# Three expert tiles that start from six batches' routing, the earliest one's layer 1 queued around the last router's steps

## The chip, the cores and the metric

One core of a Trainium2 chip runs one program that holds attention, routing and a mixture of experts. The metric is the device time of one execution in microseconds, as the median of several runs. The engines named below are PE (TensorE, matmuls; it loads weights on a track of its own), DVE (VectorE), ACT (ScalarE), POOL (GpSimd) and SP (SyncE, which here only issues DMAs).

## The reference

```
# q, k, v: 8 batches x 8 heads x 1152 x 64
q_pool = q.reshape(B, H, 576, 2, 64).mean(axis=3)
attn   = softmax(q_pool @ k^T / 8)            # 576 x 1152 for each head
x      = (attn @ v) laid out as 4608 tokens x 512
logits = x @ w_gate                            # 8 experts
e      = argmax(logits, axis=1)                # one expert for each token
scale  = softmax(logits)[e] * sigmoid(x @ w_output_gate)[e]
out    = scale * (relu(x @ w1[e]) @ w2[e])     # 512 -> 1024 -> 512
```

Everything is float32; the kernel keeps that precision by splitting operands into a high and a low part (`...h`, `...l`) and multiplying the parts.

## The kernel before

**Attention.** 32 pairs of heads (8 batches x 4 pairs) go through PE one after another. For each pair there is a pass for the row maxima (`mp`), then 18 score tiles (`sps`), each turned on ACT into `p` and `ph`, and on POOL or DVE into the remainder `pl` (L411, L405), then P V (`av`, L426 to L428). DVE normalises the result into `xb` (`norm`, L435 to L437). After each pair, `logits` transposes that part of `xb` (L481), splits it and multiplies it with the gate weights (L498). After a batch's fourth pair, `router` finds the expert of each of its tokens: transposes of the logits (L523), a softmax on DVE, a rank within the expert by matmuls with a triangle and with the running counts `cum` (L555 to L558), a position (`posi`), the new `cum` (L592), a write of the token rows to DRAM (`wr`, L580), and five scattered DMAs on POOL that write the tokens' ids into a table by expert (L597).

**Early choice.** After the sixth batch's router `setup` picks full tiles of 256 tokens for the experts that have most tokens so far: it runs `P1` rounds of small DVE steps with a PSUM bank held, and then gathers their ids (L746) and the rows of the first of them (L757). `P1` is 2 here. These are the tiles -2 and -1.

**Experts.** 22 tiles run in order: -2, -1, then 13 slots of 256 tokens (D), 4 of 192 (T) and 3 of 128 (S). Which expert each of the late ones has is known only after the last router: `totals1` sums the counts on PE, `totals2` and `table` work out the tiles on DVE, `fill` writes the experts for the weight loads, `gid` and `gat` gather ids and rows on POOL. For a tile of 256 tokens:

- `split1`, `split2` split the raw weights W1 and W2 (`raw1`, `raw2`, loaded by SP, two sets a and b used in turn) into `w1h`, `w1l` (L905, L906) and `w2h`, `w2l` (L911, L912): a cast on ACT, then a subtraction on DVE or POOL.
- `xt` transposes the gathered rows on PE (L924) and splits them (L930, L931) into `x`.
- Layer 1 has four groups of 16 matmuls (`l1m`, L944), each into one of two PSUM tiles `hps`. After each, ACT copies one half out (L957) and DVE adds the other (L958), and `relu` makes `hh` on ACT and `hl` on DVE (L964, L965), usually one group later.
- Layer 2 is two halves of 24 matmuls (`l2`, L985 to L988); DVE scales the result (`y`, L999), POOL scatters it to the output.

**Order.** In attention the order on PE, DVE, ACT and POOL is that of the code (`manual_schedule`), and so it is for the tiles on PE, DVE and ACT. What lies outside, and how the two are interleaved where attention ends, is set by a planner when the program is built: it takes what is ready by its own costs, with earlier code first. `issue_after(i)` puts the instructions of a block behind `i` on its engine; `add_manual_dep(..., NoSync ...)` fixes the order of two instructions of one engine. Neither is a wait at run time. Pools of tiles lie in SBUF in the order of the code, and a tile of the experts waits until the tiles of attention that had its place are done with.

Before, the first tile's layer 1 is placed like this: all of its first group is queued ahead of the last router's rank matmul, behind its last transposes, and the other groups follow after the rank matmuls. The casts of the first tile's rows, their remainders and that group are held ahead of three of the last router's steps.

Of the kernel before, what the change touches and what calls it, by code (L numbers as in the profile page):

```python
# [37 lines left out]
SLOTS = dict(D=13, T=4, S=3)  # L38
WIDTH = dict(D=256, T=192, S=128)
DRAINS = (8, 17)  # L40
# [26 lines left out]
def attention(tc, qT, kT, vL, wg, keep, xrows, idscr, cum, pairs, setup, scat, init, exps, behind):  # L67
    nc = tc.nc
    nb = len(pairs) // 4
    with ExitStack() as ctx:  # L70
# [345 lines left out]
        def av(st, h, xb):  # L416
# [4 lines left out]
            for c in range(NC):  # L421
                ph, pl = st['ph', h, c], st['pl', h, c]
                for qb in range(5):
                    q0 = 128 * qb if qb < 4 else NQ - 128
                    hi, lo = ph[:, q0:q0 + 128], pl[:, q0:q0 + 128]
                    nc.tensor.matmul(av_[:, qb, 0:65], lhsT=hi, rhs=vt[:, h, c, 0:65], start=c == 0 and qb == 0, stop=False)  # L426
                    nc.tensor.matmul(av_[:, qb, 0:64], lhsT=hi, rhs=vt[:, h, c, 66:130], start=False, stop=False)  # L427
                    nc.tensor.matmul(av_[:, qb, 0:65], lhsT=lo, rhs=vt[:, h, c, 0:65], start=False, stop=c == NC - 1 and qb == 4)  # L428
# [43 lines left out]
        def logits(b, c, xb):  # L472
# [4 lines left out]
            for c0, c1, grp in ((0, 256, (0, 1)), (256, NQ, (2, 3, 4))):  # L477
                tx, tk = psum(True)
                for i, t in enumerate(grp):
                    x = xb[:, t, 128 * c:128 * c + 128]  # L480
                    nc.tensor.transpose(out=tx[:, 128 * i:128 * i + 128], in_=x, identity=ident)  # L481
# [27 lines left out]
        def router(b, xb):  # L509
# [11 lines left out]
            for t in range(5):  # L521
                q0 = 128 * t if t < 4 else NQ - 128
                lt = nc.tensor.transpose(out=tl[:, 32 * t:32 * t + 32], in_=lT[:, q0:q0 + 128], identity=ident[0:32, 0:32])  # L523
# [3 lines left out]
            late = [V.tensor_copy(out=lh, in_=tv[:, :, 0:16])]  # L527
# [10 lines left out]
            late.append(nc.scalar.activation(out=ex[:, :, 0:8], in_=ex[:, :, 0:8], func=AF.Exp))  # L538
# [16 lines left out]
            late.append(nc.tensor.matmul(rk[:, 0:40], lhsT=tri, rhs=of, start=True, stop=False))  # L555
            for s_ in range(1, 5):
                nc.tensor.matmul(rk[:, 8 * s_:40], lhsT=ones, rhs=of[:, 0:40 - 8 * s_], start=False, stop=False)
            rl = nc.tensor.matmul(rv, lhsT=ones, rhs=cum.unsqueeze(1).broadcast_to([128, 5, 8]), start=False, stop=True)  # L558
            if b == nb - 1:
                behind.extend(i.ins for i in late + [lt, rl])  # L560
# [7 lines left out]
            V.tensor_tensor(out=r1, in0=rv, in1=eoff, op=ALU.add)  # L568
# [130 lines left out]
def keep_tiles(tc, kp, NT, NP_):  # L699
# [15 lines left out]
    t('es', [128, 2], I32)  # L715
# [3 lines left out]
class Moe:  # L719
    def __init__(self, tc, kp, keep, xrows, idscr, cum, w1, w2, out, nb):  # L720
# [5 lines left out]
        while self.P1 < 2 and -(-(self.early - TS * self.P1) // 8) >= TS:  # L726
# [11 lines left out]
        self.behind = []  # L738
# [23 lines left out]
    def setup(self, psum, free):  # L762
# [3 lines left out]
        if not P1:  # L766
            V.memset(k['oh1'], 0.0)
            V.memset(k['ef'][:, 0:2], 0.0)
            V.memset(k['es'], 0)
            return  # L770
# [9 lines left out]
        for i in range(P1):  # L780
# [10 lines left out]
            V.tensor_scalar(out=k['ef'][:, i:i + 1], in0=mi, scalar1=8.0, scalar2=None, op0=ALU.add)  # L791
# [12 lines left out]
            else:  # L804
                V.tensor_copy(out=k['oh1'], in_=oh)
                if P1 > 1:
                    V.scalar_tensor_tensor(out=cn, in0=oh, scalar=-float(TS), in1=cn, op0=ALU.mult, op1=ALU.add)
# [11 lines left out]
    def run(self):  # L819
# [3 lines left out]
        with ExitStack() as ctx:  # L823
# [8 lines left out]
            ma = pool("m_a")  # L832
            mx = pool("m_x")
            wq = pool("m_wq")
# [50 lines left out]
            if P1:  # L885
                e = nc.sync.value_load(k['es'][0:1, 0:1], min_val=0, max_val=7)
                wload(0, bass.ds(e, 1))
            else:
                wload(0, slice(0, 1))
            if P1 > 1:  # L890
                e = nc.sync.value_load(k['es'][0:1, 1:2], min_val=0, max_val=7)
                lastw = [wload(1, bass.ds(e, 1))]
            else:
                lastw = [wload(1, slice(0, 1))]
# [13 lines left out]
            def split2(t, c):  # L908
# [3 lines left out]
                V.tensor_tensor(out=W2[1][:, z], in0=raw[:, z], in1=W2[0].bitcast(F32)[:, z], op=ALU.subtract)  # L912

            def xt(t):
# [4 lines left out]
                xe = ps_h[1].tile([128, 2, 512], F32, name="hps") if t < -1 else None  # L919
# [14 lines left out]
            def l1m(t, g):  # L934

                d = T_[t]
                hp = ps_h[g % 2].tile([128, 2, 512], F32, name="hps")
                w = width(t)
                for f in range(2):
                    fs = slice(128 * f, 128 * f + 128)  # L940
                    for c in range(4):
                        for l in (0, 1) if c == 0 else (1, 0):
                            n = w if l else 2 * w
                            d['mm'] = nc.tensor.matmul(hp[:, f, 0:n], lhsT=W1[l][g][:, c, fs], rhs=d['x'][:, c, 0:n], start=c == 0 and l == 0, stop=c == 3 and l == 0)  # L944
                return hp

            def l1(t, g, hp=None):
# [8 lines left out]
                hs = m1.tile([128, 2, TS], F32, name="hs", bufs=2)[:, :, 0:w]  # L956
                nc.scalar.copy(out=hs, in_=hp[:, :, w:2 * w])  # L957
                V.tensor_tensor(out=hs, in0=hp[:, :, 0:w], in1=hs, op=ALU.add)  # L958
# [49 lines left out]
            def totals1():  # L1008
                cp = z['cp'] = ps_y.tile([128, 512], F32, name="cp", tag="yp")
                nc.tensor.matmul(cp[:, 0:8], lhsT=k['ones'], rhs=self.cum, start=True, stop=True)  # L1010

            def totals2():
# [13 lines left out]
                z['D'] = table('D', NT, nt, TS, eo, 2)  # L1026
                next(z['D'])

            def totals2s():
                rem = m1.tile([128, 8], F32, name="rem")  # L1030
# [69 lines left out]
            def totals3():  # L1100
                run_(z['D'])
                fill('D', 0)

# [25 lines left out]
            def first():  # L1129
                for t in range(2 - max(P1 - 1, 0)):  # L1130
                    gid(t)
                    gat(t)
                if P1 < 2:
                    loads(0)
                if not P1:
                    loads(1)

            order = list(range(-P1, NU))

            def tile_(i, t, u, pre):  # L1140

                acts = []
                early = t < -1
# [169 lines left out]
```

## Time and profile before

| | |
|---|---|
| median of 3 runs | 1494.16 us (1493.35 to 1494.33) |
| profiled execution | 1494.86 us, span 1493.1 us, mean granted clock 0.997 |
| PE busy | 1461.7 us, 98% of the span |
| DVE, ACT, POOL busy | 1104.3, 1124.7, 1025.1 us |
| DMA | 265.97 MB, 178 GB/s in the mean |

Times in the lists are microseconds from the start of the span. A list of instructions gives the start, the duration, the engine, the line of the kernel, the operation, the tile written and those read, the shape, how many were merged into the row (`x8`), and in brackets the idle time of the engine just before and what ended it. Matmuls overlap in the lists, so what counts for PE is the distance from one start to the next. The attention part ends near 1008 us; 1008 to 1066 is the seam in which the last router, the two early tiles and the choice of the late ones lie.

### The profile page before, as it was taken

How to read it: one execution, taken by the hardware profiler on the slowest of the kernel's cores; microseconds unless marked ns; L12 is line 12 of the kernel's file. 1: busy time of each engine (PE TensorE's matmuls, PEld its weight loads, DVE VectorE, ACT ScalarE, POOL GpSimd, SP SyncE). 2: the span in 40 equal slices, each digit the busy share in tenths (PEclk: the TensorE clock that was granted, in tenths of full speed). 3: DMA queues.
4: the chain of work that ended last, by engine and by line, in shares of the span. 5: the costliest groups of instructions: out<-in, count | busy, mean ns of one | idle time of the engine just before them, and what ended most of it. 6: DMA issues, size and time to landing. Idle time of an engine off the chain costs nothing.

```text
span 1493.1 us, 40870 instructions
## 1 busy us (share of the span) xinstructions
PE 1461.7 (98%) x15806; PEld 1330.7 (89%) x15806; DVE 1104.3 (74%) x2374; ACT 1124.7 (75%) x1957; POOL 1025.1 (69%) x900
## 2 busy tenths in 40 slices
PE   7999999999999999999999999999999999999998
PEld 6999999999999999999999899987888888888985
DVE  7677777777777777777777777748888778777863
ACT  6888888888888888888888788884656556556662
POOL 5887889789889879888988898886533323333420
PEclk9999999999999999999999999999999999999999
DMA  5577567656567457755766555444966666666751
GB/s 172 147 179 193 134 157 175 169 136 166 146 163 189 124 137 170 177 148 130 178 168 162 152 136 146 112 147 136 374 244 232 232 240 213 240 234 231 263 211 63
DMA packets 96708, 265.97 MB, mean 178 GB/s; under 512 B 12826, under 2 KB 17066, under 8 KB 96498
## 3 DMA queue, kind: packets, MB, share of 16 engines
q1 hardware_dynamic: 85994, 241.52, 56.0%
q0 software_dynamic: 9088, 20.86, 4.0%
q8 instruction: 129, 2.11, 0.6%
q10 hardware_dynamic: 1424, 0.88, 0.2%
q14 instruction: 73, 0.60, 0.1%
HBM read 160.04 MB, written 22.50 MB: 122 GB/s over the span
## 4 chain that ended last, share of the span: by engine, by line
PE 92%; DVE 4%; DMA 1%; ACT 1%; issue 1%; POOL 1%; ACTq 0%; POOLq 0%; SPq 0%; DVEq 0%
PE mp L332 21%; PE hps L944 15%; PE sps L395 12%; PE sps L397 10%; PE av L426 6%; PE av L427 6%; PE av L428 6%; PE yp L985 4%; PE yp L986 4%; PE yp L988 4%; DVE pm L333 1%; PE tp L481 1%; PE tp L498 1%; PE xps L924 1%; PE yp L983 1%
## 5 line engine op out<-in xcount | busy, mean ns | idle before, releaser
L333 DVE TENSOR_REDUCE pm<-mp 128x1 f32<-128x384 f32 x864 | 452.8, 550 | 210.3 <-PE mp L332 209.5
L411 POOL TENSOR_TENSOR pl<-p,ph 128x576 f16<-128x576 f32 x386 | 493.8, 1285 | 135.0 <-ACT ph L410 103.4
L409 ACT ACTIVATE p<-sps 128x576 f32<-128x576 f32 x386 | 253.0, 655 | 88.7 <-PE sps L397 66.1
L332 PE MATMUL mp<-ka,qa 128*128 128x384 f32 x960 | 314.5, 344 | 0.8 <-DVE lT L502 0.6
L426 PEld LDWEIGHTS <-ph 128*128 128x128 f16 x2880 | 261.9, 96 | 39.4 <-issue 27.7
L426 PE MATMUL av<-vt,ph 128*128 128x65 f16 x2880 | 294.3, 193 | 0.0
L427 PE MATMUL av<-vt,ph 128*128 128x64 f16 x2880 | 292.3, 194 | 0.0
L428 PE MATMUL av<-vt,pl 128*128 128x65 f16 x2880 | 291.5, 192 | 0.0
L395 PE MATMUL sps<-qa,ka 128*128 128x288 f32 x1152 | 276.6, 321 | 4.3 <-DVE pl L405 3.4
L427 PEld LDWEIGHTS <-ph 128*128 128x128 f16 x2880 | 264.7, 97 | 0.8
L428 PEld LDWEIGHTS <-pl 128*128 128x128 f16 x2880 | 265.0, 99 | 0.0
L332 PE MATMUL mp<-kb,qb 66*128 66x384 f32 x768 | 260.4, 339 | 0.6 <-DVE kb L206 0.6
L410 ACT ACTIVATE ph<-sps 128x576 f16<-128x576 f32 x386 | 251.0, 650 | 0.0
L397 PE MATMUL sps<-qb,kb 68*128 68x288 f32 x1152 | 246.4, 296 | 1.0 <-DMA qb<-mr 1.0
L944 PE MATMUL hps<-x,w1h 128*128 128x512 f32 (+2 forms) x704 | 224.4, 382 | 0.6 <-DVE x L931 0.6
L395 PEld LDWEIGHTS sps<-qa,ka 128*128 128x128 f32 x1152 | 183.1, 190 | 7.3 <-DVE pl L405 1.9
L397 PEld LDWEIGHTS sps<-qb,kb 68*128 68x128 f32 x1152 | 185.0, 189 | 1.3 <-issue 1.2
L332 PEld LDWEIGHTS mp<-ka,qa 128*128 128x128 f32 x960 | 178.0, 190 | 3.1 <-DVE pm L333 2.0
L944 PE MATMUL hps<-x,w1l 128*128 128x256 f32 (+2 forms) x704 | 162.8, 272 | 0.0
L957 ACT COPY hs<-hps 128x512 f32<-128x512 f32 (+2 forms) x88 | 47.4, 539 | 147.9 <-PE hps L944 147.8
L405 DVE TENSOR_TENSOR pl<-sps,ph 128x576 f16<-128x576 f32 x190 | 143.6, 756 | 15.8 <-ACT sps L402 14.8
L401 ACT ACTIVATE ph<-sps 128x576 f16<-128x576 f32 x190 | 124.6, 656 | 38.1 <-PE sps L397 30.2
(271 smaller groups left out, 2948.1 us busy)
## 6 DMA issues: line engine op xcount, KB each, us to landing
ka<-xk SPq DMA_DIRECT2D x120, 288.0 KB
raw1a<-in_w_dram SPq DMA_DIRECT2D x22, 1024.0 KB
raw2a<-in_w_dram SPq DMA_DIRECT2D x22, 1024.0 KB
raw1b<-in_w_dram SPq DMA_DIRECT2D x22, 1024.0 KB
raw2b<-in_w_dram SPq DMA_DIRECT2D x22, 1024.0 KB
vp<-in_vL_dram SPq DMA_DIRECT2D x32, 576.0 KB
qp<-in_qT_dram SPq DMA_DIRECT2D x31, 576.0 KB
kpf<-in_kT_dram SPq DMA_DIRECT2D x31, 576.0 KB
```

The source lines that it names most:

```text
L332: nc.tensor.matmul(mp, lhsT=l, rhs=r, start=j == 0, stop=j == len(ops) - 1)
L333: nc.vector.tensor_reduce(out=pm[:, i:i + 1], in_=mp, axis=AX.X, op=ALU.max)
L395: nc.tensor.matmul(sps[:, j, 0:288], lhsT=ka[:, h, ks], rhs=qa[:, o + 288 * j:o + 288 * j + 288], start=True, stop=False)
L397: nc.tensor.matmul(sps[:, j, 0:288], lhsT=kb[:, h, ks], rhs=qb[:, h, 288 * j:288 * j + 288], start=False, stop=True)
L405: nc.vector.tensor_tensor(out=pl.rearrange("p (j n) -> p j n", j=2), in0=x, in1=ph2, op=ALU.subtract)
L409: nc.scalar.activation(out=p32.rearrange("p (j n) -> p j n", j=2), in_=x, func=AF.Exp, scale=1.0 / 16)
L410: e_ = nc.scalar.activation(out=ph2, in_=x, func=AF.Exp, scale=1.0 / 16)
L411: nc.gpsimd.tensor_tensor(out=pl, in0=p32, in1=ph, op=ALU.subtract)
L426: nc.tensor.matmul(av_[:, qb, 0:65], lhsT=hi, rhs=vt[:, h, c, 0:65], start=c == 0 and qb == 0, stop=False)
L427: nc.tensor.matmul(av_[:, qb, 0:64], lhsT=hi, rhs=vt[:, h, c, 66:130], start=False, stop=False)
L428: nc.tensor.matmul(av_[:, qb, 0:65], lhsT=lo, rhs=vt[:, h, c, 0:65], start=False, stop=c == NC - 1 and qb == 4)
L944: d['mm'] = nc.tensor.matmul(hp[:, f, 0:n], lhsT=W1[l][g][:, c, fs], rhs=d['x'][:, c, 0:n], start=c == 0 and l == 0, stop=c == 3 and l == 0)
```

## The change

`P1` becomes 3, and the D slots become 12, so there are again 22 tiles: -3, -2, -1, then 12 + 4 + 3. `setup` runs three rounds and gathers ids for three tiles.

For the earliest tile (`head`, t = -3): its transposes use the first of the two `hps` tiles and its groups the other one first; group 0 is queued on PE behind the last P V and ahead of the last router's transposes; group 1 behind the transposes of the logits and ahead of the rank matmul; groups 2 and 3 behind the rank matmuls. On DVE the adds of groups 0 and 1 are ahead of the router's `lg` and `r1`. The relus of groups 0 and 1 run in the steps of groups 2 and 3, so two are left for after layer 1. The first two of its W2 splits go to POOL, and all four of the next tile's W1 splits to DVE (two before layer 2, two after it).

The routing of the late tiles (`chain`: totals, table, `fill`, ids and rows of tile 0) runs piece by piece in the second tile. The third tile's weights are loaded with its early choice, without that routing. The rows of the second and third tile are gathered without waiting in code order for the router; pools `mh` (for `hs`) and `me` (for the second tile's rows) are new, and `m_wq` stands ahead of `m_x`.

```diff
-SLOTS = dict(D=13, T=4, S=3)
+SLOTS = dict(D=12, T=4, S=3)
...
-        while self.P1 < 2 and -(-(self.early - TS * self.P1) // 8) >= TS:
+        while self.P1 < 3 and -(-(self.early - TS * self.P1) // 8) >= TS:
...
@@ setup
+            if i < P1 - 1:
+                yield
+                V.scalar_tensor_tensor(out=cn, in0=oh, scalar=-float(TS), in1=cn, op0=ALU.mult, op1=ALU.add)
...
@@ run
             ma = pool("m_a")
+            wq = pool("m_wq")
             mx = pool("m_x")
-            wq = pool("m_wq")
+            mh = pool("m_h")
+            me = pool("m_e")
...
             def loads(t, **kw):
                 with tc.issue_after(lastw[0].ins):
+                    if t < 0:
+                        e = nc.sync.value_load(k['es'][0:1, t + P1:t + P1 + 1], min_val=0, max_val=7)
+                        lastw[0] = wload((t + P1) % 2, bass.ds(e, 1))
+                        return
...
-                xe = ps_h[1].tile([128, 2, 512], F32, name="hps") if t < -1 else None
+                xe = ps_h[0].tile([128, 2, 512], F32, name="hps") if t == -P1 else None
...
-                hp = ps_h[g % 2].tile([128, 2, 512], F32, name="hps")
+                hp = ps_h[(g + 1) % 2].tile([128, 2, 512], F32, name="hps")
...
+            def chain():
+                totals2()
+                yield
+                yield from table('D', NT, z['nt'], TS, z['eo'], 2)
+                yield
+                fill('D', 0)
+                yield
+                gid(0)
+                gat(0)
+                yield
+                yield from totals2s()
...
@@ tile_
-                    if acts:
+                    if acts and not (head and g < 2):
                         acts.pop(0)()
                     if g == 0 and pend:
                         pend.pop(0)()
+                    if head:
+                        with tc.issue_after(hooks[('av', 'lt', 'ranked', 'ranked')[g]].ins):
+                            hp = l1m(t, g)
+                        acts.append(l1(t, g, hp))
+                        if g < 2:
+                            before(hooks[('xb', 'rank')[g]], d['mm', g])
+                            before(hooks[('lg', 'r1')[g]], d['add', g])
+                        if g == 2:
+                            totals1()
+                        with tc.issue_after(self.exps[-2]):
+                            split2(t, g, nc.gpsimd if g < 2 else V)
+                    else:
+                        acts.append(l1(t, g))
                     if halves(t) == 1:
                         acts.pop(0)()
+                    if t == 1 - P1:
+                        next(late)
...
                 for c in range(4):
-                    if u is not None:
-                        split1(u, c, nc.gpsimd if early and c > 1 else V)
+                    if u is not None and not (head and c > 1):
+                        split1(u, c)
                     if acts:
                         acts.pop(0)()
...
                 if u is not None and halves(t) > 1:
                     xt(u)
+                for c in (2, 3) if head else ():
+                    split1(u, c)
...
@@ before the tiles
+            self.gather(1 - P1, me, 1, self.early)
+            with tc.issue_after(self.exps[-2]):
+                split1(order[0], 0, nc.gpsimd)
+            with tc.high_priority():
+                cast = xt(order[0])[1]
+            for c in range(1, 4):
+                with tc.issue_after(cast.ins):
                     split1(order[0], c, nc.gpsimd)
+            self.gather(2 - P1, mg, 3, self.early)
```

`hooks` holds the last instance of each named instruction of attention and of the last router; `before(late, early)` orders two instructions of one engine.

More of the change, by code (lines that the diff above doesn't have):

```diff
@@ L64, in make_lower, with attention @@
     nc.gpsimd.affine_select(out=tri, in_=tri, pattern=[[1, 128]], compare_op=ALU.is_gt, fill=0.0, base=0, channel_multiplier=-1)
-def attention(tc, qT, kT, vL, wg, keep, xrows, idscr, cum, pairs, setup, scat, init, exps, behind):
+def attention(tc, qT, kT, vL, wg, keep, xrows, idscr, cum, pairs, setup, scat, init, exps, hooks):
     nc = tc.nc
@@ L480, in logits @@
                     x = xb[:, t, 128 * c:128 * c + 128]
-                    nc.tensor.transpose(out=tx[:, 128 * i:128 * i + 128], in_=x, identity=ident)
+                    t_ = nc.tensor.transpose(out=tx[:, 128 * i:128 * i + 128], in_=x, identity=ident)
+                    if c0 == 0 and i == 0:
+                        hooks['xb'] = t_
                 d = 0
@@ L554, in router @@
             of = ohb.rearrange("p t e -> p (t e)")
[L555 removed]
+            hooks['rank'] = nc.tensor.matmul(rk[:, 0:40], lhsT=tri, rhs=of, start=True, stop=False)
             for s_ in range(1, 5):
                 nc.tensor.matmul(rk[:, 8 * s_:40], lhsT=ones, rhs=of[:, 0:40 - 8 * s_], start=False, stop=False)
[L558 to L560 removed]
+            hooks['ranked'] = nc.tensor.matmul(rv, lhsT=ones, rhs=cum.unsqueeze(1).broadcast_to([128, 5, 8]), start=False, stop=True)
             sl = sm.tile([128, 5], F32, name="sl", bufs=2)
@@ L567, in router @@
             r1 = cut(rk, 40, 5, 8)
-            V.tensor_tensor(out=r1, in0=rv, in1=eoff, op=ALU.add)
+            hooks['r1'] = V.tensor_tensor(out=r1, in0=rv, in1=eoff, op=ALU.add)
             r2 = sm.tile([128, 5, 8], F32, name="r1", bufs=2)
@@ L737, in __init__ @@
         self.exps = []
-        self.behind = []
+        self.hooks = {}
     def gather_ids(self, t, idx, pool, bufs):
@@ L765, in setup @@
         V = nc.vector
[L766 to L770, printed above, removed]
+        assert P1 == 3
         yield
@@ L1127, in gat, with before, tile_ @@
                     self.gather(t, mg, 3, self.NTOK + 1)
[L1129 to L1136, printed above, removed]
             order = list(range(-P1, NU))
-            def tile_(i, t, u, pre):
+            hooks = self.hooks
+            def before(late, early):
+                tc.add_manual_dep(late.ins, early.ins.name, mybir.DependencyInfo(mybir.DependencyClass.NoSync, mybir.DependencyReason.DATA), reason="early tile in between")
+            def tile_(i, t, u):
                 acts = []
-                early = t < -1
+                head = t == -P1
+                d = T_[t]
                 for g in range(4):
-                    if halves(t) > 1 and not early:
+                    if halves(t) > 1 and not head:
                         with tc.issue_after(self.exps[-1]):
                             split2(t, g)
-                    if acts:
+                    if acts and not (head and g < 2):
                         acts.pop(0)()
@@ L1187, in tile_ @@
                     loads(t + 2)
-                if not early:
+                if not head:
                     gat(t + 3)
@@ L1278, in body @@
         pairs = [(b, hp) for b in range(nb) for hp in range(4)]
-        attention(tc, qT, kT, vL, wg, keep, xrows, idscr, cum, pairs, m.setup, m.scat, init, m.exps, m.behind)
+        attention(tc, qT, kT, vL, wg, keep, xrows, idscr, cum, pairs, m.setup, m.scat, init, m.exps, m.hooks)
         m.run()
```

102 lines of the change are left out of this document (28 added, 74 removed).

## The prediction

> **What bounds the kernel now.** I read the page first, then the granted clock and busy time of single stretches, then the instruction lists of TensorE (PE), ScalarE (ACT), VectorE (DVE) and GpSimd (POOL) between the last P V and the first tile whose tokens all eight batches decide.
>
> ```profile
> PE 1461.7 (98%) x15806; PEld 1330.7 (89%) x15806; DVE 1104.3 (74%) x2374; ACT 1124.7 (75%) x1957; POOL 1025.1 (69%) x900
> ```
>
> PE is the bound, 98% busy. Both kernels run 22 expert tiles of the same widths (2 early + 13 + 4 + 3 before, 3 early + 12 + 4 + 3 after), so no matmul goes away: only time in which PE stands, or runs slowly, can. The stretches (columns: length, busy time of PE, PE weight load, DVE, ACT, POOL, then clock, DMA share, GB/s):
>
> ```profile
> 844.00:846.00 2.00, 0.75 (x8) 0.41 (x7) 1.97 (x8) 1.76 (x4) 1.86 (x4) 1.00 0.78 183
> 1008.60:1012.00 3.40, 2.32 (x10) 1.31 (x10) 2.88 (x7) 1.30 (x5) 3.40 (x2) 1.00 1.01 396
> 1012.00:1018.80 6.80, 6.58 (x29) 5.40 (x29) 2.66 (x13) 1.60 (x4) 2.84 (x2) 0.50 0.54 201
> 1032.50:1035.90 3.40, 1.98 (x13) 1.24 (x11) 3.33 (x4) 1.53 (x2) 3.38 (x3) 1.00 0.43 129
> 1007.98:1065.96 57.98, 53.50 (x261) 43.25 (x262) 49.89 (x110) 31.12 (x45) 39.67 (x27) 0.94 0.60 215
> ```
>
> From 1012.0 to 1018.8 the clock is granted at one half, although PE works. The last row is the whole seam: 57.98 us from the end of the last P V to layer 1 of the first late tile. Its landmarks on PE (start, duration, line, operation; in brackets the idle time before):
>
> ```profile
> 1005.34 1.09 PE L924 MATMUL hps<-ident,xg 128*128 128x128 f32 x8 [0.47 <-DVE pl L405]
> 1007.79 0.19 PE L428 MATMUL av<-vt,pl 128*128 128x65 f16 x1
> 1009.05 0.77 PE L481 MATMUL tp<-ident,xb 128*128 128x128 f32 x5 [1.07 <-DVE xb L437]
> 1013.05 0.80 PE L944 MATMUL hps<-x,w1h 128*128 128x512 f32 x1
> 1018.35 0.26 PE L555 MATMUL tp<-ohb,tri 128*128 128x40 bf16 x1
> 1018.58 0.59 PE L944 MATMUL hps<-x,w1h 128*128 128x512 f32 x1
> 1027.34 0.39 PE L985 MATMUL yp<-w2h,hh 128*128 128x512 f32 x1
> 1032.18 0.50 PE L988 MATMUL yp<-w2h,hl 128*128 128x512 f32 x1
> 1033.64 0.66 PE L924 MATMUL xps<-ident,xg 128*128 128x128 f32 x4 [0.27 <-DMA xg<-xrows,ids]
> 1035.46 0.66 PE L924 MATMUL xps<-ident,xg 128*128 128x128 f32 x4 [1.16 <-DMA xg<-xrows,ids]
> 1035.87 0.48 PE L985 MATMUL yp<-w2h,hh 128*128 128x512 f32 x1
> 1041.48 0.50 PE L944 MATMUL hps<-x,w1h 128*128 128x512 f32 x1
> 1060.01 0.66 PE L924 MATMUL xps<-ident,xg 128*128 128x128 f32 x4 [1.02 <-DMA xg<-xrows,ids]
> 1065.96 0.39 PE L944 MATMUL hps<-x,w1h 128*128 128x512 f32 x1
> ```
>
> and from the chain of waits the price of a whole layer 1 at full clock:
>
> ```profile
> 1066.12 11.25 PE hps L944 x64
> ```
>
> So a group of 16 matmuls costs 11.25/4 = 2.81 us (I take 2.85), half a layer 2 (24 matmuls) 1041.48 - 1035.87 = 5.6 less the first's start-up, 5.5 (0.228 each), a token transpose about 0.9. The first layer-1 group, at half clock, took 1013.05 to 1018.35: 5.3 us. Work that must be done in the seam: 64 + 64 layer-1 matmuls 22.6, four halves of layer 2 22.0, two transposes 1.8, the router's own small matmuls about 1.9 (0.77 and 0.23 from rows here, 0.9 my estimate for the logits): 48.3. So 57.98 - 48.3 = 9.7 us are lost: 1.07 for the normalisation, some 2.5 in the router's steps from 1009.05 to 1013.05, 2.5 to half clock, 0.3 at 1032.18, 1.4 to 1.7 and 1.0 to 1.2 to the three gather waits. That is all that the change can win here.
>
> **The change part by part.**
>
> *1. Inputs of the earliest tile.* The transposes now go to the other score bank pair (that of the last but one score tile), which the exps before the one of L402 free, not to the one that waited for pl at L405: the 0.47 us goes; I take 0.35, since the remaining P V must still follow pl. In code order the pool of x0 now stands behind that of w2l; adding up tile sizes, x0 leaves the place of the last ph/pl tiles for that of kp, long free.
>
> ```profile
> 1003.79 0.65 ACT L402 ACTIVATE sps<-sps 128x576 f32<-128x576 f32 x1
> 1004.36 2.92 ACT L905 CAST w1h<-raw1a 128x1024 fp32r<-128x1024 f32 x3
> 1008.06 0.59 ACT L930 CAST x<-hps 128x512 fp32r<-128x512 f32 x1 [0.77 <-POOL w1l L906]
> 1005.47 7.00 POOL L906 TENSOR_TENSOR w1l<-raw1a,w1h 128x1024 fp32r<-128x1024 f32 x3 [0.37 <-ACT w1h L905]
> 1021.28 1.06 POOL L597 DMA_INDIRECT idscr<-tid,posi  x1 [3.48 <-DVE cum L592]
> 1027.54 1.49 POOL L597 DMA_INDIRECT idscr<-tid,posi  x1 [0.30 <-issue]
> ```
>
> Before, the x cast began at 1008.06, 0.08 us after the last P V ended (1007.79 + 0.19): I read that as the wait that goes. After, ACT ends its exps at 1004.44 and has one W1 cast (0.97) and two x casts (0.55 each) to do. If the W1 cast is first, POOL's first split (7.00/3 = 2.33) ends at 1007.8 as now and group 0 follows the P V within 0.1. If the x casts are first, the split ends at 1008.9 and group 0 waits about 1.0. I take the middle, 0.55.
>
> *2. Group 0 ahead of the last router.* 2.85 us of matmuls cover the normalisation: its 1.07 is saved. The router's transposes are queued behind them and start about 1.8 us later than now.
>
> *3. Groups 1 to 3.* From the router's first transposes to layer 1 it takes 1013.05 - 1009.05 = 4.0 us; nothing was put into that stretch, and I keep 4.0. Group 1 then covers the softmax steps on DVE as the first group does now. At full clock it takes 2.85 where that took 5.3. Rank matmuls 0.23 (1018.35 to 1018.58). After them:
>
> ```profile
> 1018.78 0.21 DVE L568 TENSOR_TENSOR tp<-tp,eoff 128x40 f32<-128x40 f32 x1 [3.15 <-PE tp L558]
> 1020.81 0.17 DVE L592 TENSOR_TENSOR cum<-tp,cum 128x8 bf16<-128x8 f32 x1
> 1028.21 0.69 DVE L958 TENSOR_TENSOR hs<-hps,hs 128x512 f32<-128x512 f32 x1
> 1029.16 1.23 DVE L912 TENSOR_TENSOR w2l<-raw2a,w2h 128x1024 fp32r<-128x1024 f32 x1 [0.26 <-ACT w2h L911]
> 1030.30 1.22 DVE L906 TENSOR_TENSOR w1l<-raw1b,w1h 128x1024 fp32r<-128x1024 f32 x1
> 1031.44 0.68 DVE L965 SCALAR_TENSOR_TENSOR hl<-hs,hh 128x512 fp32r<-128x512 f32 x1
> ```
>
> The step at L568 now stands behind group 1's add (0.69, behind ACT's copy), 1.3 us after that group ends. From L568 to cum takes 1020.98 - 1018.78 = 2.2, so cum comes 3.5 us after group 1, while rank and group 2 fill 0.23 + 2.85: with its own hops the totals matmul, queued behind group 2, makes PE wait 0.6 before group 3. From group 0's start to the end of layer 1: 2.85 + 4.0 + 2.85 + 0.23 + 2.85 + 0.6 + 2.9 = 16.3 us.
>
> *4. A new stall in the earliest tile's layer 2.* The relus of groups 0 and 1 now run one step later, so two, not one, are left when layer 1 ends. DVE's order there, from layer 2's start L (1027.34 now): w2l ends at L + 2.96, w1l at L + 4.1, hl of group 2 at L + 4.8, the second w1l at L + 5.85, hl of group 3 at L + 6.55. PE wants them with its 15th and 21st matmul, at L + 3.2 and L + 4.56. Now hl of group 3 comes at 1032.12 = L + 4.8 and PE waits 0.28. After: 1.65 for the first, then 0.4 for the second: half a layer 2 takes 5.5 + 2.05. I set nothing against it: both W2 splits given to POOL (2.4 each) hide in the 6 us of idle time before the scatters at 1021.28.
>
> *5. Gathers and weights.* Tile two's rows land in a place that qp leaves early, tile three's no longer under the last batch's xb: the waits of 0.27 and 1.16 go. The late tile is now the fourth, so the routing chain, ids, gather and its weights (SP's queue, issued after the chain) have one tile of 23 us more; the 1.02 goes. Tile three's weights are queued on SP without the routing; their second half waits there for the W2 split, with the last xrows write ahead of it if the queue follows readiness. Two gathers of ids and four of rows move on POOL into attention; an indirect DMA holds POOL 1.06 to 1.49 us. If they fall into POOL's 31% idle time they cost 0, if all four row gathers fall into the last pl steps about 5; I take 0, as their places come free tens of microseconds before the end.
>
> *6. The routing chain.*
>
> ```profile
> 1033.36 2.13 DVE L1017 CAST nr<-ni 128x8 f32<-128x8 int32 x1
> 1038.27 0.07 DVE L1050 MEMSET taD<- 128x8 f32 x1
> 1039.30 0.17 DVE L1062 SCALAR_TENSOR_TENSOR vAD<-tsD,eo 128x8 f32<-128x8 f32 x1
> 1041.34 0.29 DVE L1069 TENSOR_TENSOR geD<-Tn,tbD 128x136 f32<-128x136 f32 x1
> 1042.91 0.30 DVE L1079 TENSOR_REDUCE AD<-geD 128x17 f32<-128x136 f32 x1
> ```
>
> It moves into the second tile's four groups: totals (six steps at 0.2 = 1.2), first table part 1039.47 - 1038.27 = 1.2, two more 1042.91 - 1041.34 = 1.57. With 1.13 for w2l, 0.62 for hl and 0.6 for the add, DVE needs 3.5 us a group against PE's 2.81, falls behind, and hl of group 3 is ready 5.8 us into layer 2, wanted at 4.56: a stall of 1.3. Two weight splits return from POOL to DVE behind it, within DVE's slack until the third tile. L1017 took 2.13 us beside POOL's split; after, POOL has none there.
>
> *7. Third round of the early choice.* One more round of DVE steps, and a PSUM bank held for that round too.
>
> ```profile
> 854.94 1.02 DVE L799 TENSOR_TENSOR tp<-ohe,oh 128x8 f32<-128x8 f32 x1
> 857.12 1.27 DVE L803 TENSOR_TENSOR oh<-oh,ohe 128x8 f32<-128x8 f32 x1
> ```
>
> The second round had these two long steps without PE loss; the first, beside the next batch's logits, lost 1.25 us (844 to 846). Bounds 0 and 1.25; it is nearest to the second, I take 0.2.
>
> **The sum.** After, from the last P V: wait 0.55, layer 1 with the router 16.3, layer 2 7.55, transpose 0.9, 5.5, layer 1 11.3, 6.8, 0.9, 5.5: 55.3, against 57.98: 2.7 less; with 0.35 from part 1 and 0.2 against, 2.8 us, to which I hold. The profiled execution took 1494.86 (span 1493.1), 0.7 above the median of 1494.16; 1494.16 - 2.8 = **1491.4**.
>
> **The rivals.**
>
> *The half clock stays.* The router's 4 us still hold only about 1.3 us of matmuls. The stretch 1008.6 to 1012.0 was followed by half clock, 1032.5 to 1035.9 (with two gather waits) was not, so the bar lies near what group 0 leaves behind it. Where the clock drops, group 1 and part of group 2 run at half rate: 1.3 to 2.5 us lost again, about 1493.4. For it: the stretch is nearly as long; against: it is now framed by dense groups. [...]
>
> *POOL serves the scatters first (slower).* The planner orders POOL. If the five scatters (1021.28 to 1029.03) are queued ahead of both W2 splits, these end at 1031.4 and 1033.8, while layer 2 wants them from about 1024.7 and 1026.1: 6.7 us of stall and then 1.0, which swallow the 2.05 of part 4, 5.7 net: 1497.1. It decides from the point where w2h's casts come later than posi. Against: by the steps above the first W2 cast is ready some eight microseconds before posi, the second 1.4 before. With only the second late it is 5.3 - 2.05 = 3.3 us: 1494.7.
>
> *The DVE stalls don't come.* If PE's order or DVE's slack hides parts 4 and 6, 3.3 us return less what is late next: about 2 us, 1489.4. For it: PE shows only 0.28 us now; against: DVE's order is fixed.
>
> **How the numbers follow.** Forecast 0.42 (own range 1490.2 to 1492.6, the two ACT orders and part 7), half clock 0.25, stalls hidden 0.16, POOL 0.17, with the gathers that hold up the last pl (5 us, 1496.4) counted in it. Range 1489.2 to 1495.9, which leaves out the far end of each side. 0.2% (3 us, about what this measurement can tell from no change) puts the bound of faster at 1491.2, inside the forecast: a little over half of it and the hidden case are faster, 0.40; the rest of it, the half clock and the mild POOL case the same, 0.46; the far POOL case, whose price of 5.7 lies at the bound and grows with each longer scatter, slower, 0.14.
>
> **What would show it.** Group 0 (L944's successor) right behind the last L428; no half clock after it; a totals matmul with about 0.6 us before it; two waits on hl in the first layer 2; no gather wait at the second and third token transposes; the seam at 55 us for its first two tiles. Wrong if the clock column shows a half again, if a w2l on POOL stands behind the scatters, or if PE loses more behind 858 than now.

## The result, and the profile after

The changed kernel takes 1505.28 us (median of six runs, 1504.05 to 1506.97) against 1494.24 for the kernel before beside it (1493.35 to 1496.88): ratio 1.0072, 95% interval 1.0059 to 1.0085. It is 11.0 us slower; the forecast was 1491.4. The profiled execution took 1506.97, span 1505.2, against a span of 1493.1: 12.1 us are to be found.

First the page, then stretches of the trace of the kernel after (length, busy time of PE, PE weight load, DVE, ACT, POOL, then the granted clock, which is the share of its full speed that PE was given, DMA share, GB/s):

```profile
PE 1469.2 (98%) x15806; PEld 1333.0 (89%) x15806; DVE 1102.8 (73%) x2389; ACT 1125.4 (75%) x1957; POOL 1027.3 (68%) x900
...
908.00:912.00 4.00, 1.09 (x16) 1.00 (x13) 1.61 (x5) 3.48 (x8) 4.00 (x3) 0.78 1.02 242
912.00:916.00 4.00, 4.00 (x18) 3.75 (x18) 2.31 (x7) 2.35 (x6) 4.00 (x4) 0.50 0.40 86
1014.97:1074.62 59.65, 53.70 (x261) 43.25 (x262) 43.87 (x97) 31.82 (x46) 28.85 (x20) 0.94 0.55 181
1022.77:1027.23 4.46, 4.46 (x18) 3.73 (x17) 2.17 (x11) 0.44 (x2) 3.08 (x2) 0.62 0.63 214
1033.68:1044.04 10.36, 7.68 (x25) 5.31 (x24) 7.21 (x8) 4.97 (x7) 7.54 (x6) 0.84 1.02 277
```

The number of matmuls is the same, and PE is busy 7.5 us longer for them: part of the loss is work that runs more slowly, at half clock or otherwise. Three places share the loss.

**Attention.** A mark in time that both traces have is the first step of the normalisation on DVE (L435), once for each pair of heads. The rows of before, then of after:

```profile
865.19 0.23 DVE L435 TENSOR_SCALAR r<-av,sc 128x5 f32<-128x5 f32 x1 [0.45 <-PE av L428]
883.41 0.21 DVE L435 TENSOR_SCALAR r<-av,sc 128x5 f32<-128x5 f32 x1
945.19 0.21 DVE L435 TENSOR_SCALAR r<-av,sc 128x5 f32<-128x5 f32 x1
```

```profile
865.37 0.22 DVE L435 TENSOR_SCALAR r<-av,sc 128x5 f32<-128x5 f32 x1
884.95 0.21 DVE L435 TENSOR_SCALAR r<-av,sc 128x5 f32<-128x5 f32 x1
952.94 0.21 DVE L435 TENSOR_SCALAR r<-av,sc 128x5 f32<-128x5 f32 x1
```

The same work takes 19.58 in place of 18.22 us in the first stretch (1.36 more) and 67.99 in place of 61.78 in the second (6.21 more). The first holds the third round of the early choice:

```profile
871.19 2.64 POOL L234 TENSOR_TENSOR kp<-kpf,xk 128x1152 fp32r<-128x1152 f32 x1
...
871.37 2.49 DVE L800 TENSOR_TENSOR oh<-oh,ohe 128x8 f32<-128x8 f32 x1
...
874.31 0.62 PE L332 MATMUL mp<-ka,qa 128*128 128x384 f32 x2 [1.16 <-DVE xl L490]
```

An addition of 8 elements holds DVE for 2.49 us, up to the end of POOL's subtraction beside it (871.37 + 2.49 and 871.19 + 2.64); what DVE does for the running pair comes behind it, and PE waits 1.16. This cause is read from the rows; no run moves that addition away from POOL's step. In the second stretch, POOL, ACT and PE in turn:

```profile
902.15 1.10 POOL L757 DMA_INDIRECT xg<-xrows,ids  x1 [0.15 <-PE mp L332]
903.55 1.01 POOL L757 DMA_INDIRECT xg<-xrows,ids  x1 [0.30 <-issue]
907.08 1.42 POOL L237 TENSOR_TENSOR yq<-qp 128x576 f32<-128x576 f32 x1
...
903.82 0.70 ACT L410 ACTIVATE ph<-sps 128x576 f16<-128x576 f32 x1
908.52 0.67 ACT L240 CAST xq<-yq 128x576 fp32r<-128x576 f32 x1 [4.01 <-POOL yq L237]
...
911.29 0.82 PE L395 MATMUL sps<-qa,ka 128*128 128x288 f32 x2 [2.91 <-DVE xl L490]
```

The row gather stands on POOL right ahead of `yq`, the pooled queries of the next pair. ACT reaches its cast of them and stands for 4.01 us, with all exps queued behind; PE runs out of work (1.09 us of it in 908 to 912) and then goes on at half clock (0.50 in 912 to 916). The row of PE names `xl` on DVE as what came last; that waits for a cast `xh`, which stands on ACT behind the one of `xq`. In the kernel before, POOL was all but full in that pair of heads already (length, then busy times in the order above, POOL's the fifth):

```profile
885.00:900.00 15.00, 15.00 (x231) 14.43 (x231) 9.85 (x23) 12.78 (x23) 14.92 (x14) 1.00 0.50 169
```

**The seam**, PE's landmarks after:

```profile
1014.78 0.19 PE L428 MATMUL av<-vt,pl 128*128 128x65 f16 x1
1016.25 0.47 PE L942 MATMUL hps<-x,w1h 128*128 128x512 f32 x1 [1.29 <-DVE r L435]
1019.14 0.60 PE L481 MATMUL tp<-ident,xb 128*128 128x128 f32 x4
1022.77 0.72 PE L942 MATMUL hps<-x,w1h 128*128 128x512 f32 x1
1030.75 0.18 PE L1008 MATMUL cp<-cum,ones 128*128 128x8 bf16 x1 [0.33 <-DVE cum L592]
1033.68 0.39 PE L983 MATMUL yp<-w2h,hh 128*128 128x512 f32 x1
1038.65 0.50 PE L983 MATMUL yp<-w2h,hh 128*128 128x512 f32 x1 [1.89 <-ACT hh L962]
1040.17 0.79 PE L986 MATMUL yp<-w2h,hl 128*128 128x512 f32 x1 [0.79 <-DVE hl L963]
1044.04 1.03 PE L922 MATMUL xps<-ident,xg 128*128 128x128 f32 x8
1067.11 0.50 PE L986 MATMUL yp<-w2h,hl 128*128 128x512 f32 x1 [0.59 <-DVE hl L963]
1074.62 0.39 PE L942 MATMUL hps<-x,w1h 128*128 128x512 f32 x1
```

From the end of the last P V (1014.78 + 0.19) to layer 1 of the third tile it takes 59.65 us, where before took 57.98: 1.67 more, not 2.7 less. Group 1 (1022.77 to 1027.23) took 4.46 at clock 0.62; the first half layer 2 (1033.68 to 1044.04) took 10.36, with two waits and a mean clock of 0.84. What group 0 waits for (the idle time of 1.29 ends with the second half of the first tile's rows in `x`), and why the relus are late, is seen on ACT, then DVE:

```profile
1014.80 0.58 ACT L928 CAST x<-hps 128x512 fp32r<-128x512 f32 x1 [0.76 <-DVE x L929]
1032.11 0.59 ACT L955 COPY hs<-hps 128x512 f32<-128x512 f32 x1 [2.62 <-DVE hl L963]
1037.02 1.05 ACT L903 CAST w1h<-raw1b 128x1024 fp32r<-128x1024 f32 x1
1037.97 0.63 ACT L962 ACTIVATE hh<-hs 128x512 fp32r<-128x512 f32 x1
...
1015.42 0.69 DVE L929 TENSOR_TENSOR x<-hps,x 128x512 fp32r<-128x512 f32 x1 [0.65 <-ACT x L928]
1030.62 1.41 DVE L963 SCALAR_TENSOR_TENSOR hl<-hs,hh 128x512 fp32r<-128x512 f32 x1
1039.43 0.68 DVE L963 SCALAR_TENSOR_TENSOR hl<-hs,hh 128x512 fp32r<-128x512 f32 x1
```

ACT casts the second half only after DVE has the remainder of the first, and the second remainder ends at 1016.11, 0.14 before group 0 starts. The copy of group 2 needs one of the two `hs` buffers, and those are held until the postponed `hl` of group 0 is done at 1032.03. The second tile's W1 cast then stands ahead of `hh` on ACT. The row of PE at 1016.25 names L435 on DVE, which ended later still; in the built program group 0 waits for the second remainder, not for that step.

**Every tile behind the seam.** The next two rows are layer 1 starts ten tiles behind those at 1065.96 (before) and 1074.62 (after), then groups of layer 2 matmuls between 1100 and 1300 (before L986, after L984), and one layer 1 in the chain of waits of after:

```profile
1296.29 0.39 PE L944 MATMUL hps<-x,w1h 128*128 128x512 f32 x1
...
L986 PE MATMUL yp<-w2l,hh 128*128 128x512 f32 x144 | 56.1, 389 | 0.0
```

```profile
1307.23 0.40 PE L942 MATMUL hps<-x,w1h 128*128 128x512 f32 x1
...
L984 PE MATMUL yp<-w2l,hh 128*128 128x512 f32 x135 | 53.5, 396 | 0.0
...
1237.61 11.20 PE hps L942 x64
```

A tile takes 230.33 / 10 = 23.03 us before and 232.61 / 10 = 23.26 after (called the period of a tile below), with no wait, at full clock (from 1100 to 1300 PE is busy for 200.00 us at clock 1.00 in both), and with layer 1 if anything quicker (11.20 against 11.25). Layer 2's matmuls are slower, each a little, from the first to the last (a half takes 5.59 and 5.68 us in place of 5.45 and 5.55). With the last tiles that makes 3.4 us. The account of the 12.1 us: 0.2 up to 865, 1.36 and 6.21 in the two stretches, then 0.76 gained up to the end of the last P V, 1.67 in the seam, 3.4 behind it.

### The profile page after: what moved, and what is told of

Read it like the earlier page. It is cut to its first block, busy times and chain, and to the rows that moved or that the text cites. A ratio compares the mean times of both kernels' runs of the same rounds, so it can differ in the third digit from the quotient of the medians.

```text
span 1505.2 us, 40876 instructions
## 1 busy us (share of the span) xinstructions
PE 1469.2 (98%) x15806; PEld 1333.0 (89%) x15806; DVE 1102.8 (73%) x2389; ACT 1125.4 (75%) x1957; POOL 1027.3 (68%) x900
## 4 chain that ended last, share of the span: by engine, by line
PE 91%; DVE 4%; ACT 1%; DMA 1%; issue 1%; POOL 1%; ACTq 0%; POOLq 0%; SPq 0%; DVEq 0%
PE mp L332 20%; PE hps L942 14%; PE sps L395 11%; PE sps L397 10%; PE av L426 6%; PE av L427 6%; PE av L428 5%; PE yp L983 5%; PE yp L984 5%; PE yp L986 4%; DVE pm L333 1%; PE tp L481 1%; PE xps L922 1%; PE tp L500 1%; DMA qb<-mr 1%; PE yp L981 1%
```

## The experiments

The tables below use the two stretches of attention (from L435 near 865 to that near 884, and on to that near 946) and the tile period, read in each kernel's own trace as above.

### What delays attention

Theory: POOL's additional gathers make it late for `yq` (and `pl`). Rivals: only the phase of the row gather matters, or the third round on DVE.

The kernel after with the row gather later:

```diff
-        for _ in range(8):
+        for _ in range(17):
             yield
         self.gather(-P1, kp, 1, self.early)
```

> The kernel after, with its setup gather of token rows issued 17 steps behind the third round instead of 8, so that it meets the pair of attention at about the point where the kernel before had it. Theory: 5 to 6 of the 7.66 us that attention lost come from the gather's two issues on POOL falling just ahead of the yq sums on which ACT's exps and then PE wait (window 902 to 916 us). It expects the last score near 1005 us, no granted clock under 0.9 between 900 and 920 us, and a time near 1499.5 us. Rival: the third round and the longer hold of the PSUM bank cost attention its time wherever the gather stands; then attention still ends near 1010 us and the time stays above 1503 us.

Measured: 1500.45 us, 1.0046 of before (1.0029 to 1.0063). The last score came at 1003.87 in place of 1010.43. The loss in the second stretch falls to 0.9 us, with the third round still there, so the round is not what costs the second stretch.

The same step late in the kernel before:

> The kernel before with nothing of the change but its setup gather 9 steps later (17 in place of 8 behind its second round), which is the delay that a third round of 8 steps and two more id gathers bring in the kernel after. Theory: the gather's phase in the pair of attention alone costs 5 to 6 us; it expects 1499 to 1500.5 us with a half clock just behind the gather. Rival: it takes the third round as well; then within 1 us of 1494.2.

Measured: 1495.65 against 1495.1, ratio 1.0011 (0.9996 to 1.0025). The theory in this form fell: the gather's two issues stand 4.93 us ahead of `yq` as they do in the kernel after, and ACT does not wait. What differs is that POOL comes to that point on time: ACT's `ph` ahead of the cast starts at 903.70 there and 903.82 in the kernel after, the gather at 897.23 and 902.15. So the phase is not enough by itself; the next kernel leaves the phase as the change has it and moves two pairs of id gathers:

```diff
         for i in range(P1):
-            self.gather_ids(i - P1, ris[i], kp, P1)
+            if not i:
+                self.gather_ids(i - P1, ris[i], kp, P1)
             yield
...
         self.gather(-P1, kp, 1, self.early)
+        for i in range(1, P1):
+            for _ in range(9):
+                yield
+            self.gather_ids(i - P1, ris[i], kp, P1)
```

> The kernel after with the row gather where it is, but the two id gathers of the second and the two of the third tile issued 9 and 18 steps behind it in place of ahead of it; all steps between are kept. Theory: POOL was late for yq because eight indirect gathers fell into one pair of attention; with four of them ahead of yq it is not late, the wait of 4.01 us on ACT for yq goes and the half clock behind it, and attention ends 5 to 6 us sooner (last score near 1005 us, time near 1499.5). Rival: the place of the row gather just ahead of yq is enough to stop ACT, however many id gathers stand ahead of it; then attention ends near 1010 us and the time stays above 1503.

Measured: 1500.03, 1.0036 (1.0019 to 1.0053), 5.3 us less than the change. In its trace the row gather is issued at 897.88, still right ahead of `yq`; the rows of POOL, ACT, and the stretch behind:

```profile
902.80 1.42 POOL L237 TENSOR_TENSOR yq<-qp 128x576 f32<-128x576 f32 x1
...
904.99 0.73 ACT L240 CAST xq<-yq 128x576 fp32r<-128x576 f32 x1
...
908.00:912.00 4.00, 4.00 (x69) 3.90 (x69) 3.12 (x10) 3.68 (x8) 4.00 (x5) 1.00 0.92 221
```

ACT does not wait, PE is busy throughout at full clock. Now the reverse: the kernel before with POOL's six id gathers and no third round.

```diff
+        for _ in range(8):
+            yield
-        for i in range(P1):
-            self.gather_ids(i - P1, ris[i], kp, P1)
+        for i in (0, 1, 1):
+            self.gather_ids(i - P1, ris[i], kp, P1 + 1)
             yield
```

> The kernel before with POOL's part of the change alone and no third round: behind its two rounds it waits 8 steps more, then issues six id gathers in place of four (the second tile's ids twice), and 8 steps later the row gather, as the kernel after does. Theory: eight indirect gathers on POOL in one pair of attention, the last just ahead of yq, are enough; it expects yq about 5 us late, a wait of some 4 us on ACT for it with a half clock behind, attention ending 5 to 6 us later and a time of 1499 to 1500.5. Rival: the third round's steps on DVE (its 2.49 us beside POOL, its wait ahead of mp) are part of it; then 1496 or less, and no wait over 1.5 us for yq.

Measured: 1502.63, 1.0052 (1.0035 to 1.0068), more than expected. Rows of its POOL and PE, and two stretches:

```profile
893.46 5.00 POOL L411 TENSOR_TENSOR pl<-p,ph 128x576 f16<-128x576 f32 x4
...
894.79 0.20 PE L428 MATMUL av<-vt,pl 128*128 128x65 f16 x1 [1.14 <-POOL pl L411]
...
892.00:896.00 4.00, 2.09 (x33) 1.63 (x33) 1.65 (x4) 1.79 (x4) 3.63 (x5) 0.95 0.04 6
896.00:900.00 4.00, 4.00 (x37) 3.89 (x37) 2.37 (x5) 3.19 (x6) 4.00 (x4) 0.63 0.01 4
```

The gathers alone are enough, but the place that was expected was wrong: most is lost right behind the id gathers (the last at 892.39), where POOL has four `pl` steps to catch up on (5.00 us in a row) and P V waits 1.14 us for one; ACT waits only 0.92 us for `yq`. The second stretch takes 5.4 us more than in the kernel before. About 3 us more of the profiled execution's time lie in its first 100 us, where the clock was 0.94 between 50 and 100; nothing in the edit touches that, and it stays open. So 5.4 us of the 8.4 by the medians are accounted for.

| kernel | rounds | id gathers, row gather at | first stretch | second stretch |
|---|---|---|---|---|
| before | 2 | 4 at 863 to 869, 882 | 18.22 | 61.78 |
| before, row gather later | 2 | 4 at 865 to 871, 897 | 18.20 | 61.74 |
| before, six id gathers | 2 | 6 at 881 to 893, 906 | 17.60 | 67.16 |
| after | 3 | 6 at 877 to 889, 902 | 19.58 | 67.99 |
| after, row gather later | 3 | 6 at 875 to 888, 913 | 19.60 | 62.72 |
| after, ids moved | 3 | 2 ahead, 898, then 4 | 19.57 | 61.76 |

The first stretch goes with the rounds (1.4 us for the third), the second with what POOL issues in it and when. In the changed kernel it takes both parts: the six id gathers with the row gather later lose 0.9 us, the row gather ahead of `yq` without four of them nothing. In the kernel with six id gathers, where the last of these comes 5.0 us behind the step near 884 and not 3.2, most is lost before the row gather is issued.

### What slows layer 2

An unused tile of 32 bytes ahead of all, as the kernel after has all its expert tiles 32 bytes off a multiple of 64:

```diff
     t('oh1', [128, 8], F32)
+    t('pad', [128, 8], F32)
```

> The kernel after, with an unused 32-byte tile among the small kept tiles, so that every later SBUF tile lies 32 bytes higher: the start addresses of w2l, w2h, hh and hl are again multiples of 64, as in the kernel before (in the kernel after they are 32 above one). Theory: the 3.33 us that were lost behind the third tile are layer 2's matmuls at a slower cadence because of the odd 32 bytes. It expects a D tile's period of 23.04 us again in place of 23.27, an hh.w2h cadence of 0.232 us, and a time 3.0 to 3.5 us under the kernel after's, near 1502. Rival: the cadence follows from which tile lies where (pools were reordered) or from something else than the address modulo 64; then the period stays 23.27 us and the time at 1505.

Measured: 1505.0, 1.0077 (1.0055 to 1.0099), and a period of 23.26. The theory fell. Together with the later gather:

> The kernel after with both edits: gather 17 steps behind the third round, and the 32-byte tile. Theory: the two losses are apart in time and add up: 1495.5 to 1497 us, of which the seam's 1.7 us over the kernel before stays. Rival: at least one of the two is not the cause; then not under 1499 us.

Measured: 1499.38, 1.0033 (1.0018 to 1.0048), with the same slow period: what the gather's move gives, no more.

The second theory is the distance of tiles to each other. The rows of the second tile (`me`, two tiles of 2080 bytes) now lie between `w2l` and the raw weights, so `w2h` has moved by an odd 64 bytes against `hh`. The kernel before with such a hole:

```diff
+            pool("m_hole").tile([128, 16], F32, name="hole")
             wa = pool("m_wa")
```

> The kernel before with a hole of 64 bytes ahead of the raw weights, so that w2h lies 122944 bytes above hh and no longer 122880 (15 times 8192), as it lies 131136 (16 times 8192 and 64) above it in the kernel after; nothing else is changed. Theory: layer 2's cadence follows from the distance of w2h and the raw weights to hh, hl and w2l, by those 64 bytes. It expects a D tile's period of 23.27 us in place of 23.04 and 3 to 3.5 us more, near 1498. Rival: the distance does not matter in this way (some other difference of the two kernels slows layer 2); then 23.04 us and no change of time.

Measured: 1497.92 against 1494.71, 1.0018 (1.0007 to 1.0030). Layer 1 starts ten tiles apart:

```profile
1065.77 0.39 PE L945 MATMUL hps<-x,w1h 128*128 128x512 f32 x1
...
1298.40 0.39 PE L945 MATMUL hps<-x,w1h 128*128 128x512 f32 x1
```

232.63 / 10 = 23.26. The other way, in the kernel after `me` goes to the top of SBUF:

```diff
-            me = pool("m_e")
...
             wp2 = pool("m_w2")
+            me = pool("m_e")
```

> The kernel after with the gathered rows of its second tile moved from below the raw weights to the top of SBUF: w2h again lies a multiple of 4096 bytes above hh, hl and w2l (126976, 118784, 110592). Theory of the distance: the period of a D tile falls from 23.27 to 23.04 us. Rival: it stays 23.27. The head of the expert part may wait for attention's buffers at the top, so only the period is read from this run.

```profile
1071.65 0.39 PE L942 MATMUL hps<-x,w1h 128*128 128x512 f32 x1
...
1302.03 0.39 PE L942 MATMUL hps<-x,w1h 128*128 128x512 f32 x1
```

230.38 / 10 = 23.04, in a single run of 1500.58. Shown from both sides: the layout alone makes 0.23 us a tile. Which sizes of a hole matter is told by two more in the kernel before, of 1024 and 256 bytes (`[128, 256]`, `[128, 64]`):

> The kernel before with a hole of 1024 bytes in the same place as the 64: only a D tile's period is read. If distances that differ by 1024 are as good as those that differ by 4096, 23.04 us; if it takes a multiple of 2048 or more, 23.2 or so.

> The same with a hole of 256 bytes. If the matter is one of the address modulo 128 or 256, 23.04 us; if of a larger block, 23.2 or so.

Both have a period of 23.04 (single runs of 1495.61 and 1494.19). So a hole of 64 bytes costs, of 256 and of 1024 nothing; 128 was not tried. The hole moves the raw weights, W1 and `w2h` together against `hh`, `hl`, `x0` and `w2l`, so which pair of tiles disturbs which is not separated. Nor is the distance separated from the moved tiles' own addresses: in the built programs `w2h` starts 64 or 96 bytes above a multiple of 256 in every layout with a period of 23.04, and 128, 160 or 192 above one in every layout with 23.26, which would fit as well. The 32-byte tile rules out only that a multiple of 64 is enough.

### What stalls the first half layer 2

```diff
-                hs = mh.tile([128, 2, TS], F32, name="hs", bufs=2)[:, :, 0:w]
+                hs = mh.tile([128, 2, TS], F32, name="hs", bufs=3)[:, :, 0:w]
...
-                    yt = my.tile([128, 512], F32, name="y", bufs=4)[0:p]
+                    yt = my.tile([128, 512], F32, name="y", bufs=3)[0:p]
...
+                if head:
+                    while acts:
+                        acts.pop(0)()
                 for c in range(4):
```

> The kernel after with the first tile's last two relus ahead of the second tile's layer 1 splits on ACT and DVE, and three hs buffers in place of two (one y buffer less pays for the room). Theory: the stalls of 1.89 and 0.79 us in the first half layer 2 and the half clock that follows come from hs copies that wait for a postponed hl and from relus queued behind splits; it expects that half to take 6 to 7 us in place of 10.36 and the time to fall by 3 to 4 us, to about 1501.5. Rival: w2l's last split on DVE is what is late, or the half clock comes anyway; then it still takes over 9 us.

Measured: 1505.33, 1.0063 (1.0045 to 1.0080): no gain. But the half layer 2 did what was expected, and the loss is elsewhere; the start of group 0, and the stretch of the half layer 2:

```profile
1018.88 0.47 PE L942 MATMUL hps<-x,w1h 128*128 128x512 f32 x1 [3.10 <-DVE x L929]
...
1037.54:1043.61 6.07, 5.84 (x25) 4.38 (x24) 5.75 (x8) 4.47 (x6) 5.15 (x4) 1.00 0.91 263
```

6.07 us at full clock in place of 10.36. The smaller `y` pool let `x0` sink by 2048 bytes onto the last `pl` tile of attention: group 0 waited 3.10 in place of 1.29, and half clock followed there (from the start of group 0 to that of group 1 it took 7.76 us at a mean clock of 0.78, in place of 6.52 at 1.00). One edit alone had moved a neighbour. The third buffer and the new order were tried only together.

### The three repairs together

Ids moved, relus ahead with three `hs` buffers (their pool now below `w2l`, so `x0` does not sink), and a hole of 960 bytes, which makes `w2h` lie a multiple of 1024 above `hh`.

```diff
+            mh = pool("m_h")
             wq = pool("m_wq")
             mx = pool("m_x")
-            mh = pool("m_h")
             me = pool("m_e")
+            pool("m_hole").tile([128, 240], F32, name="hole")
             wa = pool("m_wa")
```

> The kernel after with three repairs together: the second and third tile's id gathers behind the row gather; the first tile's relus ahead of the splits, with three hs buffers (now below w2l, so that x0 does not sink onto attention's pl as it did when only the buffer was added) and three y buffers; and a hole of 960 bytes ahead of the raw weights, so that w2h lies 134144 bytes (131 times 1024) above hh. Theory: the three losses are apart and add up: 5.3 for POOL's lateness, 4.2 for the first half layer 2, 3.3 for the distance if a multiple of 1024 is enough: 1492 to 1493.5 us, about 2 us under the kernel before, with a D tile's period of 23.04. Rival: the distance must be a multiple of 2048 or 4096; then the period stays 23.26 and the time is 1495.5 to 1497. Rival to the sum: a wait that these stalls hid takes their place; then over 1497.

Measured: 1491.57 us (median of 12 runs, 1489.52 to 1499.06) against 1494.11, ratio 0.9988, interval 0.9976 to 1.0001. The period is 23.04, the second stretch of attention 61.79, and the seam and its first half layer 2:

```profile
1006.95:1062.09 55.14, 51.40 (x263) 42.28 (x262) 43.51 (x97) 31.83 (x46) 29.11 (x20) 0.97 0.59 194
1025.66:1031.72 6.06, 5.75 (x25) 4.38 (x24) 5.69 (x8) 4.47 (x6) 5.15 (x4) 1.00 1.04 256
```

13.7 us less than the change by the medians: the three losses are apart and add up (5.3 + 4.3 + 3.3 = 12.9). Against the kernel before it is 2.5 us by the medians, but the interval reaches just past 1, so a gain over it is likely and not proved.

## Why the prediction was wrong

The prediction had the seam, and looked for all of the change there. Point by point:

- **Part 5, gathers on POOL: 0 taken, 6.2 measured.** The term that failed. The reason given (their places come free early) was beside the point: an indirect gather took POOL's time, 1.0 to 1.1 us each, and what counted was whether POOL still reached `yq` and `pl` in time. The prediction spread the gathers over a mean of 31% idle time, but in the pair of heads into which they now fall POOL had been busy for 14.92 of 15 us. It counted the wrong gathers, too. Of the four row gathers only two came to lie in attention (993.62 and 995.05), and no loss shows there; the loss came from the id gathers with the first tile's row gather, which they had pushed ahead of `yq`. The 5 us named for a bad case were near the price by luck: they were set on another place (the last `pl` steps) and counted as a part of a rival of 0.17.
- **Part 7, third round: 0.2 taken, bounds 0 and 1.25; 1.4 measured**, in four kernels with a third round (19.57 to 19.60) against two with two rounds (18.20 and 18.22). The third with two rounds, which has the six id gathers, took 17.60. The nearest row chosen was a round without loss; the one beside the next batch's logits was the better likeness.
- **No part at all: layer 2's pace, 3.4.** The diff shows pools moved and added, and the prediction read from them only which tile leaves whose place. That the place of tiles in SBUF changes PE's pace (23.26 us a tile in place of 23.04 with a hole of 64 bytes) no row of before could show.
- **Part 4, stall in the first half layer 2: 2.05 taken, 4.86 measured** (10.36 less 5.5). That late relus would stall it was right, the order was not: PE waited for `hh` from ACT at its 13th matmul (1.89) and for `hl` at its 15th (0.79), where the prediction had DVE alone in view and `hl` at the 15th and 21st. Two things were missed: with two `hs` buffers a postponed relu holds up the next copies, and half clock followed the waits (mean clock 0.59 from 1040.17 to 1044.04); it makes up most of the rest.
- **Part 1: 0.55 taken, 1.28 measured.** ACT took the order that the prediction priced at 0.1, with the W1 cast first (1012.01) and POOL's split done at 1015.48. What was left out is DVE: the two casts of `x` and their two remainders run in turn, and the last remainder ends at 1016.11.
- **Part 2: right.** Group 0 took 2.89 at full clock, and the normalisation ran beside it.
- **Part 3: nearly right.** Router stretch 3.63 (4.0 taken), wait at the totals 0.33 (0.6). Group 1 took 4.46 and not 2.85 (mean clock 0.62): the rival of the half clock, in part. In the kernel with the three repairs it took 4.38 at 0.63, with the ids moved 2.90 at 1.00, with the later gather and the 32-byte tile 2.91; so it costs 1.5 us when it comes. The longest single wait in the router stretch ahead of it was 0.40 us here, 0.46 with the three repairs, and 0.40 in the kernel with the later gather and the 32-byte tile, where group 1 was not slow. What decides it these rows do not show; the chance of 0.25 that the prediction gave the half clock was its author's estimate.
- **Part 6: right in kind.** Stall 0.59 (1.3 taken). As part 5 said, there is no gather wait at the second and third transposes. The rival of POOL's scatters ahead of the W2 splits did not come.

With the named losses repaired the seam took 55.14 us; the prediction said 55.3. The agreement is partly luck, as terms were off in both directions, but the seam was not where it went wrong: it went wrong by taking the POOL work that three early tiles add to attention as free where it lands, and the layout as without effect.

## What to carry to other kernels

Price a moved instruction in the stretch in which it lands, by that stretch's busy time and by what stands next in that engine's queue, not by the engine's mean over the span. Postponing a step holds its buffers for longer: count them before. After any change of pools compare the pace of an untouched loop in both traces; if it differs with no wait and at full clock, as here by 0.23 us a tile, look at where the tiles lie, and try a hole or another place.

## What the runs showed of the hardware

- **PE's pace changed with where its operands lie in SBUF.** A hole of 64 bytes between tiles took layer 2 of a tile from 10.99 to 11.27 us (its two halves 5.44 + 5.55 against 5.59 + 5.68) and layer 1 from 11.25 to 11.20. A common shift of 32 bytes in the kernel after left the period at 23.26, and with holes of 256 and 1024 bytes in the kernel before it was 23.04, as without. All three kinds of layer 2 matmul slowed down with the hole of 64 bytes, in the mean from one's start to the next between 1100 and 1300: `w2h` with `hh` from 0.227 to 0.233 us (the first of each half left out), `w2h` with `hl` from 0.229 to 0.231, and also `w2l` with `hh`, from 0.226 to 0.235, two tiles that the hole leaves in place. The runs do not tell whose accesses meet, or whether any do.
- **A small step on DVE lasted until the POOL step beside it ended.** The addition of 8 elements from two SBUF tiles took 2.49 us and ended (873.86) with the POOL step that it met (`kp`, 873.83), which had started 0.18 us earlier.
- **Half clock came within a wait of 2.91 us, and behind waits of 0.40.** The first was in attention (the clock is 1.00 between 909 and 910 and 0.62 between 910 and 911, some 2 us into the wait). The second was in group 1, behind a router stretch of 3.63 us in which PE was busy for 2.56 and whose longest single wait was 0.40. A stretch of 3.64 with the same longest wait, in the kernel with the later gather and the 32-byte tile, was followed by a group 1 of 2.91 us, so the length of the waits alone does not tell the two apart.
